# Slot means from column-tiled products, segments weighted ahead, and a written-out order of all instructions

## The chip, the cores and the metric

The kernel runs on one core of one Trainium2 chip. A core has five engines that run side by side and wait for one another through semaphores: TensorE (PE, matrix products and transposes; its weight loads are listed as PEld), VectorE (DVE), ScalarE (ACT), GpSimd (POOL) and SyncE (SP, which here only issues DMA transfers). The metric is the device time of one execution in microseconds. The median of three runs of the kernel before is 243.07 us (241.93 to 243.26).

## What is computed

```python
def mab(q, kv):                                   # softmax attention, one head
    s = scale * (q @ kv.transpose(0, 2, 1))
    s = s - s.max(-1, keepdims=True)
    a = np.exp(s)
    a /= a.sum(-1, keepdims=True) + 1e-09
    return a @ kv
h = mab(I, x)                                     # 32 inducing rows look at all of x
x = mab(x, h)                                     # every row of x looks at the 32 rows of h
...
logits = x @ phi                                  # 32 slots
d = softmax of logits over all rows               # (0)
slot_input = d.T @ x                              # 32 slot means
slot_out[e] = np.maximum(slot_input[e] @ w1[e], 0) @ w2[e]     # 8 experts, 4 slots each
c = softmax of logits over the 32 slots           # (1)
return c @ slot_out
```

x is 4 batches of 11456 rows of 128 numbers; the second part sees all 45824 rows as one. All is float32.

## The kernel before

**Tiles.** The rows of a batch are spread over 128 partitions, 90 blocks of 128 rows, and the blocks are cut into six tiles (five of 16 blocks, one of 10): 24 tiles, numbered 0 to 23, a multiple of six beginning a batch. A tile of scores is 128 partitions by 512 columns (320 for the small one): four groups of 32 partitions for the 32 inducing rows or slots, and blocks of 32 columns.

**Stages.** For each tile, group A (`group_a`) loads x (line 353) and, for 17 tiles, its transpose (line 361; for the other seven PE transposes, line 373, and ACT copies, line 381). It makes the scores of the inducing rows (`col_mm`, line 475), the running maximum (DVE line 394, ACT lines 400 and 402, a PE product with the matrix `rep`, line 407, DVE line 410), the exponentials (ACT line 415), turns them (DVE line 420, or PE and ACT in four tiles) and sums x with them (line 426: 16 products of 32 weight columns and 128 moving columns, four column tiles side by side). GpSimd rescales and adds these sums in `hz` (lines 436 and 444).

After the sixth tile of a batch `group_fin` finishes its mean: a product with `rep` that adds the four partition groups (line 482), the division on DVE (lines 486 to 488, which makes `h`), a transpose on PE (491), copies on ACT (494 and 497, `hts` and `ht`), and the product with phi (500, 504: `bdg`).

Group B (`group_b`) works on the batch's tiles again: scores against `hts` (line 475), softmax over 32 columns in `soft` (DVE transpose 523, maximum 527, POOL subtraction 531, ACT exponential 534, sums on POOL and DVE 539 to 558, POOL product 605, which gives `a2`), transpose (610), logits (613, put into `l_all` by lines 618 to 632). Three tiles form a segment, eight in all (`group_seg`): the segment's maximum (668 to 677), exponentials against it (688, with their sum in `z_l`), their transpose (694), and line 705, four products of 128 weight columns and 128 moving columns a tile, summed in PSUM tile `u` over the segment. Only its diagonal blocks of 32 by 32 are wanted: ACT copies `u` (722), POOL multiplies it by a mask (725; DVE 719 in the last segment), PE multiplies it by the batch mean `h` (728), ACT copies the result to `si_all` (731).

The small network (`group_mlp`) needs all eight segments: weights of the segments from their maxima (765, 768, 784), the denominator (772 to 792), the weights divided by it (795), eight products that add the weighted segments (801), the first layer (825: 32 products with 256 moving columns), the ReLU (831), two transposes (837, 842), the second layer (853: 64 products with 128 moving columns in two halves), a product with `rep` (863) and the copy to `srs` (866).

Group C (`group_c`) is the softmax of the logits over the slots, by `soft` again, with a transpose ahead (line 523, or in the seven tiles of list `TC` four transposes on PE, line 333, and a copy on ACT, line 336) and one behind (909). Group O (`group_o`) multiplies the slot outputs by it (926, four products a tile), copies the results (937, on ACT or DVE) and stores them (944).

**Order.** Everything is entered in a `Plan` with an engine, a cost in us and a priority. At build time `Plan.order` runs a list scheduler over this graph 24 times, forwards and backwards, keeps the order with the earliest end, and emits the instructions in it. So each engine's queue, SP's DMA queue among them, has a fixed order when the kernel runs. Warm-up products on PE fill gaps that the planner expects.

Of the kernel before, what the change touches and what calls it, by code (L numbers as in the profile page):

```python
# [8 lines left out]
F32 = mybir.dt.float32  # L9
# [6 lines left out]
S = 32  # L16
# [17 lines left out]
SEG = 3  # L34
NSEG = NT // SEG
# [5 lines left out]
}  # L41
LAG = {
    "ldn": -3.96, "ldt": -4.87, "tr": -1.2, "tre": 9.61, "a1": 0.0, "amx": -3.97, "am5": 0.0, "apm": 0.0, "ang": 2.71, "aex": -86.69, "aal": 0.3,
    "ate": 0.2, "a2": 0.4, "ahs": 5.38, "ahu": 0.6, "fin": -24.9, "b1": 9.19, "bts": 0.0, "bmx": 0.0, "bsb": 0.0, "bxp": 2.89, "bhf": 0.1,
    "bsm": 0.1, "bml": 0.2, "bta": 0.39, "c1": 0.36, "blm": 0.4, "ble": -7.69, "bch": -12.29, "bde": -24.64, "btd": -3.48, "c2": -44.1, "uf": 33.95,
    "warm": -2.57, "B": 18.08, "w": 29.25, "mlp": 8.95, "c": 70.84, "o": -0.67,
}
LAT = {("PE", "PE"): 0.0, ("ACT", "PE"): 0.27, ("DVE", "PE"): 0.26, ("DVE", "ACT"): 0.14, ("ACT", "DVE"): 0.1, ("DVE", "DVE"): 0.13, ("ACT", "ACT"): 0.05, ("Pool", "Pool"): 0.05}
LAT_OF = {"PE": 0.2, "DVE": 0.2, "ACT": 0.2, "Pool": 0.08, "DMA": 0.0}
DMA_LAT = 1.9  # L50
PASSES = 24
SEED = 0
NOISE = 0.0
BETA = 0.0
WARM = 8
WARM_PLAN = 2.3


def width(n):
    return SIZES[n % NCH] * S  # L60

# [13 lines left out]
TC = [1, 3, 6, 7, 9, 10, 15]  # L75
# [7 lines left out]

SLOPE = {"A": 0.574, "B": 0.622, "c": 0.566, "o": 2.276}


def first(p):

    return p[0] * SLOPE.get(p[1] if p[1] in SLOPE else "A", 1.0) + sum(LAG.get(x, 0.0) for x in p[1:])


ANY_ORDER = ("mm", "half")


class Plan:
# [3 lines left out]
    def __init__(self):  # L99
        self.ops, self.writers, self.readers, self.touch, self.rings = [], {}, {}, {}, {}  # L100

    def op(self, eng, cost, prio, fn, reads=(), writes=(), allocs=()):
        i = len(self.ops)
        deps = set()
        for k in reads:
            deps.update(self.writers.get(k, ()))
        for k in writes:
            deps.update(self.writers.get(k, ()))
            deps.update(self.readers.get(k, ()))
        for k in reads:  # L110
            self.readers.setdefault(k, []).append(i)
# [935 lines left out]
```

## Time and profile before

| what | us |
|---|---|
| median of three runs | 243.07 (241.93 to 243.26) |
| the profiled execution | 241.55 |
| its span, first to last instruction | 239.8 |
| busy in the span: PE, PEld | 201.4, 122.8 |
| busy in the span: DVE, ACT, POOL | 183.6, 147.0, 147.6 |
| read from HBM, written | 48.81 MB, 23.59 MB |

The profile is of one execution. Busy time of an engine is the union of its instructions. A float32 product shows as two instructions, each with a weight load of its own. The groups of instructions give a line, an engine, the tiles written and read, the shape, the count, the busy time and the mean length, and behind the second bar the idle time of the engine ahead of them and what ended it. The timeline merges like instructions that follow one another; its columns are start, length, and then the same names.

### The profile page before, as it was taken

The page shows a single profiled execution, that of the slowest core. Times are in us where ns is not written, and L with a number is a line of the kernel's source. Part 1 is how long each engine was busy: PE and PEld are TensorE (multiplying, and loading weights), DVE is VectorE, ACT ScalarE, POOL GpSimd, SP SyncE. Part 2 cuts the span into 40 slices and gives each one's busy share as a digit, 9 for nine tenths or more (in the row PEclk, how much of TensorE's full clock was granted, in tenths as well). Part 3 has the DMA queues.
Part 4 walks back from the last instruction along what each step waited for, and adds up shares of the span by engine and source line. Part 5 has one row for each costly group of instructions (what it writes and reads, how often), then busy time and mean ns, then how long its engine had stood idle before and what let it go on. Part 6 is the DMA issues. An engine that isn't in the chain of part 4 may idle for free.

```text
span 239.8 us, 5623 instructions
## 1 busy us (share of the span) xinstructions
PE 201.4 (84%) x2054; PEld 122.8 (51%) x2054; DVE 183.6 (77%) x427; ACT 147.0 (61%) x390; POOL 147.6 (62%) x237
## 2 busy tenths in 40 slices
PE   8899899699999799989999979989977968446370
PEld 8575574336655464637754654776843633211030
DVE  1125529879999699998969989994798999889650
ACT  2687594657747484586737652932259999285460
POOL 0001324979539697097961899986768887777810
PEclk9999999999999999999999999997999799575566
DMA  7999995999999969399996910000019999999977
GB/s 238 415 426 413 391 361 194 413 421 390 340 331 396 418 234 395 101 428 349 399 415 234 425 57 1 0 5 0 3 63 388 395 424 417 416 413 413 423 293 300
DMA packets 13851, 72.76 MB, mean 303 GB/s; under 512 B 1792, under 2 KB 2432, under 8 KB 6912
## 3 DMA queue, kind: packets, MB, share of 16 engines
q1 hardware_dynamic: 13392, 72.23, 76.6%
q8 instruction: 16, 0.26, 0.4%
q10 hardware_dynamic: 432, 0.18, 0.3%
q14 instruction: 11, 0.09, 0.1%
HBM read 48.81 MB, written 23.59 MB: 302 GB/s over the span
## 4 chain that ended last, share of the span: by engine, by line
PE 46%; DVE 15%; ACT 12%; DMA 10%; POOL 9%; issue 5%; ACTq 0%; POOLq 0%; SPq 0%
PE s L475 8%; DMA l_all<-xt 7%; PE po L926 7%; ACT ot L937 6%; PE ha L426 6%; PE lp L613 5%; PE tp L373 4%; PE s2p L475 4%; PE u L705 3%; DMA xt<-xt 3%; PE hpm L825 2%; ACT ct L534 2%; DVE l_all L909 2%; PE warm L317 2%; POOL ct L901 2%
## 5 line engine op out<-in xcount | busy, mean ns | idle before, releaser
L926 PE MATMUL po<-l_all,mb 32*128 32x512 f32 (+1 forms) x192 | 37.6, 783 | 16.1 <-DVE l_all L909 13.2
L937 ACT COPY ot<-po 128x512 f32<-128x512 f32 (+1 forms) x71 | 34.8, 594 | 16.8 <-PE po L926 16.4
L531 POOL TENSOR_TENSOR bt<-bt,bm 128x512 f32<-128x512 f32 (+1 forms) x24 | 23.7, 994 | 20.5 <-DVE bm L527 20.1
L926 PEld LDWEIGHTS po<-l_all,mb 32*128 32x128 f32 x192 | 17.2, 236 | 34.9 <-issue 13.6
L531 POOL TENSOR_TENSOR ct<-ct,cm 128x512 f32<-128x512 f32 (+1 forms) x24 | 23.8, 993 | 11.5 <-DVE cm L527 7.1
L705 PE MATMUL u<-d,a 128*128 128x128 f32 (+1 forms) x184 | 25.4, 281 | 0.4 <-DVE d L694 0.4
L901 POOL TENSOR_TENSOR ct<-ct,cz 128x512 f32<-128x512 f32 (+1 forms) x24 | 23.8, 1001 | 2.7 <-DVE cz L558 2.4
L705 PEld LDWEIGHTS u<-d,a 128*128 128x128 f32 (+1 forms) x184 | 22.3, 189 | 4.9 <-issue 1.0
L605 POOL TENSOR_TENSOR a<-bt,bz 128x512 f32<-128x512 f32 (+1 forms) x24 | 23.9, 995 | 1.5 <-DVE bz L558 1.2
L613 PE MATMUL lp<-a2t,bdg 128*128 128x512 f32 (+1 forms) x48 | 24.0, 594 | 0.9 <-ACT a2t L336 0.6
L394 DVE TENSOR_REDUCE m<-s 128x1 f32<-128x512 f32 (+1 forms) x24 | 15.3, 639 | 11.9 <-PE s L475 11.7
L426 PEld LDWEIGHTS ha<-xn,e 128*32 128x32 f32 x668 | 18.5, 110 | 9.0 <-issue 6.2
L426 PE MATMUL ha<-xn,e 128*32 128x128 f32 x668 | 22.8, 274 | 0.0
L436 POOL TENSOR_TENSOR hz<-hz,al 128x129 f32<-128x129 f32 x20 | 8.0, 398 | 23.2 <-ACT al L433 22.4
L475 PE MATMUL s<-xt,it_sb 128*32 128x512 f32 (+1 forms) x152 | 19.2, 577 | 2.4 <-DMA xt<-xt 1.2
L534 ACT ACTIVATE ct<-ct 128x512 f32<-128x512 f32 (+1 forms) x24 | 15.0, 629 | 9.5 <-POOL ct L531 9.5
L534 ACT ACTIVATE bt<-bt 128x512 f32<-128x512 f32 (+1 forms) x24 | 14.4, 600 | 10.3 <-POOL bt L531 10.1
L909 DVE STREAM_TRANSPOSE l_all<-ct 128x512 f32<-128x512 f32 (+1 forms) x24 | 16.0, 668 | 4.1 <-POOL ct L901 4.1
L937 DVE COPY ot<-po 128x512 f32<-128x512 f32 (+1 forms) x25 | 16.0, 645 | 3.5 <-PE po L926 3.4
L415 ACT ACTIVATE et<-s,negm 128x512 f32<-128x512 f32 (+1 forms) x24 | 15.7, 656 | 4.7 <-DVE negm L410 3.9
L688 ACT ACTIVATE dt<-l_all,negm_l 128x512 f32<-128x512 f32 (+1 forms) x24 | 16.5, 687 | 3.2 <-DVE negm_l L677 2.9
L475 PE MATMUL s2p<-xt,hts 128*32 128x512 f32 (+1 forms) x152 | 17.6, 573 | 0.0
(174 smaller groups left out, 428.2 us busy)
## 6 DMA issues: line engine op xcount, KB each, us to landing
xn<-xn SPq DMA_DIRECT2D x18, 1024.0 KB, 7.1
out<-ot SPq DMA_DIRECT2D x13, 1024.0 KB, 8.6
xt<-xt SPq DMA_DIRECT2D x11, 1024.0 KB, 8.7
w<-w SPq DMA_DIRECT2D x8, 1024.0 KB, 7.5
out<-ot SPq DMA_DIRECT2D x16, 256.0 KB, 2.8
l_all<-xt SPq DMA_DIRECT2D x3, 1024.0 KB, 8.2
out<-ot SPq DMA_DIRECT2D x6, 512.0 KB, 4.1
xt<-xt SPq DMA_DIRECT2D x3, 640.0 KB, 6.0
```

Source lines behind the costliest of these rows:

```text
L426: nc.tensor.matmul(ha[32 * q : 32 * q + 32, :P], T["e1", a][:, j * S : (j + 1) * S], T["xn", a][:, j * P : (j + 1) * P], start=j < 4, stop ...
L475: nc.tensor.matmul(dst[32 * g : 32 * g + 32, :w], lhs, src, start=True, stop=True)
L531: nc.gpsimd.tensor_tensor(tv, tv, T[k("m")][:, :nb].unsqueeze(2).broadcast_to(full), op=ALU.subtract)
L534: nc.scalar.activation(T[k("t")][:, :w], T[k("t")][:, :w], AF.Exp)
L605: nc.gpsimd.tensor_tensor(blocks(a2), blocks(t), zb, op=ALU.mult)
L613: nc.tensor.matmul(ptile("mm", ("lp", n))[:, :w], T["bdg", b], T["a2t", n][:, :w], start=True, stop=True)
L688: nc.scalar.activation(dt_[:, :v], l_of(n)[:, :v], AF.Exp, bias=negm_l[:, k : k + 1], accum_out=z_l[:, k, i : i + 1])
L705: nc.tensor.matmul(u[:m, :m], a2[:, o : o + m], d[:, o : o + m], start=i == 0 and o == offs[0], stop=i == SEG - 1 and o == offs[-1],)
L901: nc.gpsimd.tensor_tensor(blocks(t), blocks(t), zb, op=ALU.mult)
L909: nc.vector.transpose(l_of(n), T["ct", n][:, :w])
L926: nc.tensor.matmul(T["po", 4 * n + g][:, :w], T["srs",][q, :], l_of(n)[q, :], start=True, stop=True)
L937: (nc.vector.tensor_copy if dve else nc.scalar.copy)(ot[:, g * w : (g + 1) * w], T["po", m][:, :w])
```

## The change

- Line 705's product is now 16 products a tile, each with 32 weight columns and 32 moving columns, that write the wanted 32 by 32 blocks alone, into four column tiles that add up over the tile's blocks and the segment. `u` is then 128 by 32. Mask, masked copies, the product with `h` for each segment and `si_all` are gone; ACT copies `u` to `us_all` (segments 0 to 6).
- In the small network the first seven segments are weighted against their own common maximum while the eighth is still under way (e1 to e8): weights, their spread over partitions by a product with a matrix of ones, the product with `us_all`, and seven products with the `h` of the batch, added up. The last segment joins by two weights (g1 to g8). The slot means so come from two products (g7a, g7b). The denominator now divides the slot outputs in the copy to `srs` (gs) and no longer the weights.
- The first layer is split in two halves of 128 moving columns (64 products), each with a ReLU and a transpose of its own; both layers are entered in parts of six and two experts.
- `group_fin`: the sum of the denominators has its own short path (f0 to f2), the division goes into a scaled copy of `rep` (f2b), and two products with it give the transposed mean at once (f3a, f3), one from the sum of five tiles, one from the sixth tile's part. `h` is made later by a transpose and a copy (f8, f9). The GpSimd addition of the sixth tile is gone.
- In batch 0 the running maximum of group A is on DVE (one step a tile) and no longer on ACT.
- `TC` is gone: all 24 tiles of group C are transposed by DVE. The new modes of `soft` (lists `BV` to `CB`) are empty.
- `Plan` keeps only the functions; `ORDER`, a list of 1297 numbers, is the order in which they are emitted, and `WARMS` says after which of them how many warm-up products follow (ten places, 20 products in all). Ring sizes, semaphores and transfers are as before but for small tiles.

```diff
 def c2(n=n, i=i):
...
-                offs = list(range(0, w, P))
...
-                    nc.tensor.matmul(
-                        u[:m, :m], a2[:, o : o + m], d[:, o : o + m],
-                        start=i == 0 and o == offs[0], stop=i == SEG - 1 and o == offs[-1],
-                    )
+                for j in range(nb):
+                    q = slice(32 * (j % 4), 32 * (j % 4) + 32)
+                    c = slice(j * S, j * S + S)
+                    nc.tensor.matmul(u[q, :S], a2[:, c], d[:, c], start=i == 0 and j < 4, stop=i == seg - 1 and j >= nb - 4)
...
-        op("PE", 0.23, pr, f1, [("hz", b)], [("hp", b)], [("mm", ("hp", b))])
-        op("DVE", 0.65, pr, f2, [("hp", b)], [("h", b)], [("h", ("h", b))])
-        op("PE", 0.11, pr, f3, [("h", b)], [("htp", b)], [("mm", ("htp", b))])
+        op("DVE", 0.07, pr, f0, [("zc", a5), ("hz", b)], [("zt", b)])
+        op("PE", 0.22, pr, f1, [("zt", b)], [("hp", b)], [("mm", ("hp", b))], ni=4)
+        op("DVE", 0.22, pr, f2, [("hp", b)], [("rz", b)])
+        op("ACT", 0.25, pr, f2b, [("rz", b)], [("rzr", b)], [("rzr", ("rzr", b))])
+        op("PE", 0.28, pr, f3a, [("hz", b), ("rzr", b)], [("htp", b)], [("mm", ("htp", b))], ni=4)
+        op("PE", 0.28, pr, f3, [hl, ("rzr", b)], [("htp", b)], ni=4)
...
+            if mv and c:
+                nc.vector.scalar_tensor_tensor(m5[:, 0:4], mask4, T["m1", a], T["m5", a - 1][:, 0:4], op0=ALU.mult, op1=ALU.max)
+                return
...
+        def e5b():
+            nc.tensor.matmul(ptile("ha", ("wr",))[:, : K * S], ones, T["wsel",][:S, : K * S], start=True, stop=True)
+        def e5c():
+            nc.vector.tensor_tensor(T["uss",][:, : K * S], us_all[:, : K * S], T["wr",][:, : K * S], op=ALU.mult)
+        def e7():
+            sip = ptile("mm", ("sip",))
+            for t in range(K):
+                nc.tensor.matmul(sip[:, :S], T["h", SEG_AT[t] // NCH], T["uss",][:, t * S : (t + 1) * S], start=t == 0, stop=t == K - 1)
...
+        def g7a():
+            nc.tensor.matmul(ptile("mm", ("sit",))[:, :S], ident, T["sis",], start=True, stop=False)
+        def g7b():
+            nc.tensor.matmul(T["sit",][:, :S], T["h", B - 1], T["uss",][:, last], start=False, stop=True)
...
+        def g9(k, es):
+            def f():
+                hp = T["hpm", k] if es[0] else ptile("mm", ("hpm", k))
+                for e in es:
+                    for q in range(4):
+                        nc.tensor.matmul(
+                            hp[32 * q : 32 * q + 32, :P], T["z1s",][:, 32 * e : 32 * e + 32], wslice(1, e * F + (2 * q + k) * P, P),
+                            start=e == 0, stop=e == E - 1,
+                        )
+            return f
...
         def gs():
-            nc.vector.tensor_copy(T["srs",], T["sr",][:, :P])
+            nc.vector.tensor_scalar_mul(T["srs",], T["sr",][:, :P], T["rz", "l"])
...
-    order = plan.order()
-    T["plan"] = plan
     with tc.manual_schedule():
-        for i, gap in plan.gaps(order):
-            plan.ops[i][3]()
-            if gap > 0.5 and ("warm1",) in T and ("po", 0) not in T:
-                warm(("warm1",), int((gap - 0.3) / 0.215))
+        for i in ORDER:
+            plan.ops[i]()
+            if i in WARMS:
+                warm(("warm1",), WARMS[i])
```

More of the change, by code (lines that the diff above doesn't have):

```diff
@@ L1 @@
 import math
-import random
 import concourse.bass as bass
@@ L33 @@
 TB = [14, 15, 18, 19]
-SEG = 3
-NSEG = NT // SEG
+SEGS = [3, 3, 3, 3, 3, 3, 3, 3]
+SEG = max(SEGS)
+NSEG = len(SEGS)
+SEG_AT = [sum(SEGS[:k]) for k in range(NSEG)]
 RINGS = {
@@ L38, with seg_of, whole @@
     "dt": 2, "d": 3, "a2": 6, "mm": 4, "s2p": 3, "s1": 2, "u": 1, "ha": 1, "xa": 1, "xb": 1,
[2 rows of a table removed]
-}
[L42 to L54, printed above, removed]
[1 row of a table added]
+}
 WARM = 8
-WARM_PLAN = 2.3
 def width(n):
     return SIZES[n % NCH] * S
+def seg_of(n):
+    k = max(k for k in range(NSEG) if SEG_AT[k] <= n)
+    return k, n - SEG_AT[k]
+def whole(n):
+    return SIZES[n % NCH] % 4 == 0
 def valid(n):
@@ L402, in am5 @@
                 nc.scalar.mul(m5[:, 4:5], nmask0, T["negm1", b][:, c - 1 : c])
-        n5 = 5 if c else 4
+        mv = a - c in MV
+        n5 = 5 if c and not mv else 4
         def apm():
@@ L592, in pr @@
             return n, "B", o
+        mode = mode_of(n, BV, BE, BP) if whole(n) else "T"
+        turned = mode != "T"
         def b1():
-            col_mm(ptile("mm", ("s2p", n)), T["hts", b], n)
+            sp = ptile("mm", ("s2p", n))
+            col_mm(sp, T["hts", b], n)
         w = width(n)
@@ new lines, in group_mlp @@
+        op("ACT", 0.2, pe, e2, [("nmp",)], [("wl",)])
+        op("DVE", 0.09, pe, e3, [("wl",)] + [("z", n) for n in range(SEG_AT[K])], [("zw",)])
+        op("DVE", 0.09, pe, e3b, [("zw",)], [("zs",)])
+        op("DVE", 0.32, pe, e5, [("wl",), ("mb",)], [("wsel",)])
+        op("PE", 0.35, pe, e5b, [("wsel",), ("mb",)], [("wr",)], [("ha", ("wr",))], ni=4)
+        op("DVE", 0.32, pe, e5c, [("wr",), ("mb",)] + [("us", k) for k in range(K)], [("uss",)])
+        op("PE", 0.2 * K, pe, e7, [("uss",), ("mb",)] + [("h", SEG_AT[k] // NCH) for k in range(K)], [("sip",)], [("mm", ("sip",))], ni=4 * K)
@@ new lines, in group_mlp @@
+        op("ACT", 0.1, pe, e8, [("sip",)], [("sis",)])
+        ul = ("us", "last")
+        op("DVE", 0.07, pr, g1, [("ngl", K), ("nmp",)], [("nm",)])
+        op("ACT", 0.2, pr, g2, [("nm",)], [("wl2",)])
+        op("DVE", 0.09, pr, g5, [("wl2",)], [("ws2",)])
+        op("PE", 0.24, pr, g5b, [("ws2",)], [("wr2",)], [("ha", ("wr2",))], ni=4)
+        op("ACT", 0.1, pr, g5d, [("wr2",), ("mb",)], [ul])
+        op("DVE", 0.09, pr, g5f, [("wr2",)], [("sis",)])
+        op("PE", 0.25, pr, g7a, [("sis",)], [("sit",)], [("mm", ("sit",))], ni=4)
@@ L878, in group_mlp @@
         op("DVE", 0.07, pr, g6b, [], [("rz",)])
[L879 to L884 removed]
+        parts = (range(0, 6), range(6, E))
```

518 lines of the change are left out of this document (236 added, 282 removed), and 62 rows, old and new, of tables (ORDER, RINGS).

## Prediction

> **What bounds the kernel now.** I read the page first, then a table of busy times by stage, then the timeline around the two joints between stages, then groups and waits. The page's totals and slices:
>
> ```profile
> PE 201.4 (84%) x2054; PEld 122.8 (51%) x2054; DVE 183.6 (77%) x427; ACT 147.0 (61%) x390; POOL 147.6 (62%) x237
> PEclk9999999999999999999999999997999799575566
> DMA  7999995999999969399996910000019999999977
> ```
>
> PE is the fullest engine on average, but the DMA row shows three different stages: transfers almost without a pause while the tiles are loaded, none for five slices, then transfers without a pause while the output is written. The table by stage (columns: PE, PEld, DVE, ACT, POOL busy, granted clock, DMA share, GB/s):
>
> ```profile
> 0.00:40.00 40.00, 36.84 (x421) 25.40 (x421) 14.78 (x34) 25.59 (x70) 5.57 (x16) 1.00 0.90 349
> 40.00:120.00 80.00, 74.07 (x954) 44.32 (x953) 72.82 (x175) 52.13 (x164) 58.15 (x100) 1.00 0.92 354
> 120.00:152.00 32.00, 30.01 (x202) 17.87 (x198) 28.51 (x75) 17.82 (x46) 23.51 (x35) 1.00 0.53 211
> 152.00:163.20 11.20, 9.91 (x79) 9.01 (x79) 9.51 (x28) 5.10 (x17) 9.05 (x14) 1.00 0.01 3
> 163.20:176.25 13.05, 11.82 (x211) 8.20 (x210) 8.94 (x23) 4.45 (x8) 9.18 (x14) 0.87 0.01 3
> 176.25:228.00 51.75, 34.24 (x180) 16.27 (x184) 46.01 (x94) 37.84 (x79) 41.13 (x58) 0.77 0.96 389
> 228.00:239.80 11.80, 4.46 (x24) 1.77 (x24) 3.07 (x6) 4.12 (x9) 0.98 (x2) 0.64 0.76 295
> ```
>
> Two things follow. First, the first output product starts at 176.25 (its row stands below) and the span ends at 239.8, so 63.55 us follow it, with DMA at 0.96 for most of them: the output stage is paced by its stores, and the end moves with the moment T at which the output can start. Second, from 40 to 163 both PE and DVE are over nine tenths busy. DVE's work cannot be handed over by this change, so I set up the sum on DVE: T is the time that DVE works ahead of T plus the time that it idles ahead of T. Its idle time by stage is 25.2, 7.2, 3.5, 1.7 and 4.1 us, 41.7 in all, beside 134.6 us of work. A faster PE helps only as far as it takes away this idle time.
>
> **The change part by part.** *The product of the second mean* (line 705). Today 24 tiles take four 128x128 products each:
>
> ```profile
> 40.00:120.00 80.00, 12.97 (x92) 11.29 (x92) 0.00 (x0) 1.02 (x4) 1.00 0.92 354
> 64.33 1.06 PE L426 MATMUL ha<-xn,e 128*32 128x128 f32 x32
> 65.63 1.14 PE L705 MATMUL u<-d,a 128*128 128x128 f32 x8
> 66.70 0.64 PE L475 MATMUL s2p<-xt,hts 128*32 128x512 f32 x4
> 160.83 1.97 PE L801 MATMUL sit<-mb,si_all 128*128 128x32 f32 x16 [0.66 <-DVE mb L795]
> 128.57 0.16 PEld L475 LDWEIGHTS s2p<-xt,hts 128*32 128x32 f32 x8 [0.17 <-issue]
> ```
>
> One tile (8 instructions, two to a product) takes 66.70-65.63 = 1.07 us with its start, and the first row has twelve such tiles' worth of work (92 instructions, 12.97 us) in the stage from 40 to 120. The new form has 16 products a tile with 32 weight columns and 32 moving columns, four column tiles side by side. No row has this. The nearest row above is line 426: the same 16 column-tiled products, 32 instructions, with four times the moving columns, 1.06 us. That would be no gain. From below, line 801 has 32 moving columns behind 128 weight columns, 1.97/16 = 0.123 us an instruction, which the weights set; with a quarter of the columns it is 0.031, and 32 instructions take 0.98 us one behind another and 0.25 us four abreast. The last row speaks for abreast: eight such loads lie in 0.16 us. I take 0.45 us, nearer the low end for that row, with ends of 0.25 and 1.06. Relief of PE: 12 x 0.6 = 7 us from 40 to 120, and as much again up to 160.
>
> The Trainium skill ("TensorE: Matmul & The Clock Gate", the section on the 56 ns gap) states that start-to-start of matmuls never drops below about 25 ns however small they are. By that rule 32 instructions take at least 0.80 us, the relief is 12 x 0.27 = 3 us, and the sum below would give an estimated 241.2, between the forecast and the first rival. No run here shows it: the 33 ns an instruction of line 426 lie above it.
>
> *What hangs on that product.* Gone are seven masked copies on POOL, eight products with the batch mean (two instructions each), eight copies on ACT, and at the end the eight products of line 801. (The last three rows below count what lies ahead of 176.25 alone.)
>
> ```profile
> L725 POOL TENSOR_TENSOR um<-us,mask_bd 128x128 f32<-128x128 f32 x7 | 3.2, 460 | 0.3
> L728 PE MATMUL sip<-h,um 128*128 128x128 f32 x16 | 3.0, 288 | 0.2 <-DVE um L719 0.2
> L795 DVE TENSOR_SCALAR mb<-mb,rz_l 128x256 f32<-128x256 f32 x1 | 1.2, 1218 | 0.0
> L784 DVE TENSOR_TENSOR mb<-cst,wl 128x256 f32<-128x256 f32 x1 | 0.6, 590 | 0.0
> L488 DVE TENSOR_SCALAR h<-hp,rz 128x128 f32<-128x128 f32 x4 | 1.4, 351 | 0.1
> L668 DVE TENSOR_TENSOR m4b<-mx,cst 128x12 f32<-128x12 f32 x8 | 2.0, 256 | 0.0
> ...
> L527 DVE TENSOR_REDUCE cm<-ct 128x16 f32<-128x512 f32 (+1 forms) x10 | 6.4, 643 | 0.5 <-ACT ct L336 0.5
> L523 DVE STREAM_TRANSPOSE ct<-l_all 128x512 f32<-128x512 f32 (+1 forms) x5 | 3.2, 648 | 0.0
> L558 DVE RECIPROCAL cz<-cz 128x16 f32<-128x16 f32 (+1 forms) x9 | 2.0, 227 | 0.9 <-POOL cz L555 0.8
> ```
>
> DVE loses lines 795, 784 and 488, 1.2+0.6+1.4 = 3.2 us. It gains the weights of seven segments and their product (two by line 784, 1.1 us), six running maxima of the first batch, four sums of batch totals and some eight small steps (18 by about 0.2, line 668 being the upper end: 3.6 us, of which 3 ahead of T), and *seven transposes that PE made* (list TC): 7 x 0.65 = 4.6 us. Counting the table's entries, nine tiles are turned on DVE ahead of the last copy of the slot means, where the trace has five, so four of the seven count ahead of T: 2.6 us. One row maximum and one reciprocal fewer come ahead of T: -0.9. Work ahead of T: -3.2+1.1+3+2.6-0.9 = +2.6. As the small steps stand at their upper end, I take +1.8 (ends +0.8 and +2.6). Behind T: three transposes, the maximum and the reciprocal put off, 2.0+0.9 = +2.9.
>
> *The joint at 122* (batch mean). The denominator gets a path of its own, ahead of the last product, and normalising moves into a product.
>
> ```profile
> 121.87 0.85 PE L426 MATMUL ha<-xn,e 128*32 128x128 f32 x20
> 123.52 0.46 POOL L444 TENSOR_TENSOR hz<-hz,hs 128x129 f32<-128x129 f32 x1
> 125.89 0.35 DVE L488 TENSOR_SCALAR h<-hp,rz 128x128 f32<-128x128 f32 x1
> 127.83 0.20 ACT L494 ACTIVATE hts<-htp 128x32 f32<-128x32 f32 x1
> 128.58 0.64 PE L475 MATMUL s2p<-xt,hts 128*32 128x512 f32 x4
> ```
>
> From the last product's end (122.72) to the first score product of the last batch (128.58) are 5.9 us, through ACT, POOL, PE, DVE, PE and ACT. The new path keeps a copy on ACT, two products that each take one weight load, and the copy on ACT, with another tile's product and copy queued between by the table: about 3 us. The 3 us saved are worth at most the stage's DVE idle time. The same step shortens batch 0, where DVE idles from 0 to 40 for want of scores.
>
> *The layers of the small network.*
>
> ```profile
> 163.20 5.35 PE L825 MATMUL hpm<-w,ma 128*32 128x256 f32 x64
> 164.00:165.00 1.00, 1.00 (x16) 0.49 (x12) 1.00 (x3) 0.47 (x1) 0.53 (x2) 0.50 0.00 0
> 170.02 1.96 PE L853 MATMUL so<-w,ma 128*32 128x128 f32 x64
> 171.79 1.93 PE L853 MATMUL so<-w,mb 128*32 128x128 f32 x64
> 175.38 0.49 PE L863 MATMUL sr<-sos,cst 128*128 128x128 f32 x2 [1.07 <-DVE sos L860]
> 176.25 0.71 PE L926 MATMUL po<-l_all,mb 32*128 32x512 f32 x4 [0.16 <-DVE mb L866]
> ```
>
> The first layer took 5.35 us, and the granted clock was 0.50 in its middle. Split in halves of 128 columns it has the instructions of the second layer twice, 2 x 1.9 = 3.8 us at full clock, 5.4 if the clock falls again for as long. I take 5.4: PE ahead of it does thinner work than before. The 1.5 us between the layers (168.55 to 170.02) shrink, since the first half's activation and transpose run under the second half. From 163.20 to 176.25 are 13.05 us; new: 5.4+0.2+3.8 and 2.0 of the 2.5 us that today lie between the second layer's end (173.72) and 176.25, 11.4.
>
> *Moved.* All instructions come in a new order on every queue, SP's included. Loads wait for buffers that PE frees:
>
> ```profile
> SPq L361 <- PE s2p L475: 26.3, 10, 7.3
> ```
>
> so a relieved PE lets loads go sooner; the counts and sizes of the transfers stay. ACT and POOL lose more than they get, and bind nowhere ahead of T. In the table warm-up products stand at ten places; they cost PE little where it waits.
>
> **The sum.** Work of DVE ahead of T: +1.8. Idle: 0 to 40, 25.2 to 24.2 (-1.0; ends 0, -2); 40 to 120, 7.2 to 4.7 (-2.5: a third of PE's relief, for DVE is at 91% already; ends 0, -5); 120 to 152, 3.5 to 2.0 (-1.5; ends 0, -2.5); 152 to T, 5.8 to 4.3 (-1.5: by the 1.6 us of the small network; ends +1, -3). T moves by 1.8-6.5 = -4.7, to 171.6. Behind T, DVE gets 2.9 us more in a stage where it idles 51.75-46.01 = 5.7:
>
> ```profile
> 226.96 0.71 DVE L909 STREAM_TRANSPOSE l_all<-ct 128x512 f32<-128x512 f32 x1 [0.68 <-POOL ct L901]
> 229.50:231.30 1.80, 1.80 (x12) 0.55 (x7) 1.11 (x2) 1.46 (x3) 0.09 (x1) 0.50 0.14 57
> ```
>
> The stores already run dry once, for 1.8 us, because the last tiles' softmax comes late; I let that hole grow by 1.0 (ends 0 and 2.9). The span goes to 239.8-4.7+1.0 = 236.1. The profiled execution took 241.55, 1.75 more than its span, so 237.85, and the median of the runs (243.07) stands 0.6% over the profiled execution: 239.4 us. The ends of the terms add up to -11.7 and +6.5.
>
> **Rivals.** *First: PE is not relieved.* If the thin products take about 1 us, the terms of 40 to 120 and of the first half of the late stages (2.5+0.7) fall away: 239.4+3.2 = 242.6, no change that a measurement of this kernel can tell (0.5% is about what it can tell). For it: line 426 as it stands. Against: the eight loads in 0.16 us.
>
> *Second, slower: DVE becomes the wall.* If its idle time ahead of T is waiting for loads and POOL rather than for PE, the turned transposes and small steps add up without return: +2.6 ahead of T and +2.9 behind it, 248.6. It decides once DVE from 40 to 152 is over 95% busy while T has not moved; a middle case, with half of the idle time given back, is +1.8-3.2+2.9, 244.6. For it: the 91% above. Against: PE's own 93% there, with the batch joint visibly serial.
>
> *Third: the clock.* With thin products PE may be granted 0.50 through both layers: 3.8 more in the second layer and 2.2 more in the first, 6.0 on top of the forecast, 245.4, and it decides when the granted clock is under 0.7 from 163 to T. Against: the second layer ran at full clock behind a halved first.
>
> The Trainium skill (the same page, Part 1 on the clock gate) says that a window of some 3.4 us with an idle PE brings the clock to half. The row with 0.50 agrees with the half; an idle PE stood not ahead of it, for from 152 to 163.2 it was busy for 9.91 of 11.2 us.
>
> *Fourth: the order is much better than the planner's,* since it isn't bound to a rule: idle of 40 to 152 down to 2 us gives 234 or less.
>
> **Chances.** Forecast 0.50, with its neighbours from 236 to 241.8; fourth rival 0.15; first 0.15; second and third together 0.20, of which 0.03 end within the half per cent. Faster 0.65, same 0.18, slower 0.17. The range leaves out the far ends of fourth and second: 233.5 to 245.5.
>
> **What would show it.** Right: line 705's successor under 0.6 us a tile; from 40 to 152 PE clearly under 90% busy and DVE over 93%; the first output product at 170 to 173; about 64 us from there to the end. Wrong: that product near 1 us a tile; DVE as idle as before; T where it was; the layers at half clock; or a hole in the stores of over 4 us.

## The result, and the profile after

The kernel after takes 235.19 us (median of four runs, 233.12 to 237.61) against 242.50 of the kernel before on the same chip (241.33 to 243.26); the ratio is 0.967, 95% interval 0.957 to 0.978. The forecast was 239.4 with a range of 233.5 to 245.5, faster at 0.65. So sign and range held, and the gain is 7.3 us where about 3.7 were forecast. Runs of both kernels spread by 2% and more on some chips, and the ratios leave disturbed executions out, so they differ a little from those of the medians.

The profiled execution of after took 233.12 us, its span is 231.3. First the totals of its page, the granted clock and the DMA share by fortieths:

```profile
PE 195.4 (84%) x2658; PEld 108.7 (47%) x2658; DVE 188.9 (82%) x445; ACT 144.1 (62%) x376; POOL 143.3 (62%) x227
PEclk9999999999999999998599999999999995555555
DMA  7999996999999999999478950000059999999987
```

PE lost 6 us, DVE gained 5.3, and DVE's share of a shorter span went from 77% to 82%. Then the table by stage, in the columns of the prediction (stretch, its length; PE, PEld, DVE, ACT, POOL busy; granted clock, DMA share, GB/s), cut at the start of the first layer and at the first output product:

```profile
0.00:40.00 40.00, 36.31 (x416) 24.91 (x417) 17.10 (x41) 23.69 (x60) 6.57 (x18) 1.00 0.91 357
40.00:120.00 80.00, 74.97 (x1220) 41.19 (x1220) 74.92 (x179) 55.14 (x169) 57.43 (x96) 0.96 0.93 368
120.00:152.00 32.00, 29.54 (x457) 16.50 (x456) 31.75 (x83) 17.65 (x47) 25.74 (x38) 1.00 0.46 170
152.00:157.46 5.46, 5.16 (x114) 4.44 (x113) 5.46 (x19) 3.16 (x11) 3.34 (x8) 1.00 0.01 5
157.46:167.37 9.91, 9.44 (x266) 8.09 (x267) 9.09 (x26) 2.70 (x6) 8.33 (x12) 1.00 0.02 4
167.37:219.50 52.13, 34.98 (x172) 12.48 (x176) 47.41 (x97) 37.59 (x77) 40.22 (x58) 0.72 0.96 386
219.50:231.30 11.80, 5.05 (x24) 1.06 (x20) 3.19 (x7) 4.21 (x9) 1.69 (x3) 0.50 0.78 299
```

The first output product (the moment T of the prediction) comes at 167.37 in place of 176.25, 8.9 us sooner. From there to the end are 63.9 us, as before (63.55). So all of the gain lies ahead of T. DVE's idle time there, the length of a stretch less its DVE column, is now 22.9, 5.1, 0.25, 0.0 and 0.8 us, 29.05 in place of 41.7; its work is 167.37-29.05 = 138.3 in place of 134.6. From 120 us to T, DVE has hardly a gap left: 46.30 us of work in 47.37.

The timeline shows the three places on which the forecast was built. The product of the second mean, for one tile, for two tiles that follow one another, and its group (count, busy us, mean ns | idle before, releaser):

```profile
118.12 0.46 PE L716 MATMUL u<-d,a 128*32 128x32 f32 x32
149.22 0.94 PE L716 MATMUL u<-d,a 128*32 128x32 f32 x64
L716 PE MATMUL u<-d,a 128*32 128x32 f32 x720 | 10.6, 201 | 0.8 <-DVE d L706 0.4
```

A tile takes 0.46 us with its start, in place of 1.07, or 0.94/64 = 0.015 us an instruction.

The joint between the last batch's mean and its first scores:

```profile
122.55 0.85 PE L349 MATMUL ha<-xn,e 128*32 128x128 f32 x20
124.43 0.46 PE L425 MATMUL htp<-rzr,hz 128*128 128x128 f32 x2
124.73 0.39 PE L428 MATMUL htp<-rzr,hs 128*128 128x128 f32 x2
125.81 0.64 PE L401 MATMUL s2p<-xt,hts 128*32 128x512 f32 x4
```

From the end of the last product (123.40) to the scores (125.81) are 2.4 us in place of 5.9, with products of two other tiles' logits (line 619) in between.

And the small network:

```profile
157.46 3.27 PE L864 MATMUL hpm<-w,ma 128*32 128x128 f32 x112
161.03 0.64 PE L864 MATMUL hpm<-w,ma 128*32 128x128 f32 x16
161.49 1.49 PE L893 MATMUL so<-w,ma 128*32 128x128 f32 x48
163.17 0.65 PE L893 MATMUL so<-w,ma 128*32 128x128 f32 x16
163.94 1.96 PE L893 MATMUL so<-w,mb 128*32 128x128 f32 x64
166.44 0.49 PE L903 MATMUL sr<-sos,cst 128*128 128x128 f32 x2
167.37 1.14 PE L1007 MATMUL po<-l_all,mb 32*128 32x512 f32 x8 [0.22 <-DVE mb L906]
```

The first layer takes 3.27+0.64 = 3.9 us, the second runs right behind it, and the granted clock is 1.00 throughout: 9.91 us in place of 13.05.

### The profile page after: what moved, and what is told of

Its sections match the earlier page's. It is cut to its first block, busy times and chain, and to the rows that moved or that the text cites. A ratio compares the mean times of both kernels' runs of the same rounds, so it can differ in the third digit from the quotient of the medians.

```text
span 231.3 us, 6816 instructions
## 1 busy us (share of the span) xinstructions
PE 195.4 (84%) x2658; PEld 108.7 (47%) x2658; DVE 188.9 (82%) x445; ACT 144.1 (62%) x376; POOL 143.3 (62%) x227
## 4 chain that ended last, share of the span: by engine, by line
PE 37%; DVE 27%; DMA 15%; POOL 7%; ACT 6%; issue 4%; SPq 1%; ACTq 0%; DVEq 0%; POOLq 0%
PE po L1007 8%; PE s L401 7%; PE ha L349 5%; PE s2p L401 5%; ACT ot L1017 4%; DMA xt<-xt 4%; DMA l_all<-xn 4%; DMA xn<-xn 4%; DVE l_all L978 4%; PE lp L619 4%; PE tp L291 3%; DMA l_all<-xt 3%; DVE ct L476 2%; POOL a L596 2%; POOL ct L959 2%
## 5 line engine op out<-in xcount | busy, mean ns | idle before, releaser
L1007 PE MATMUL po<-l_all,mb 32*128 32x512 f32 (+1 forms) x192 | 40.0, 821 | 18.6 <-DVE l_all L978 12.2
L1007 PEld LDWEIGHTS po<-l_all,mb 32*128 32x128 f32 x192 | 13.5, 239 | 44.4 <-DVE l_all L978 22.6
L619 PE MATMUL lp<-a2t,bdg 128*128 128x512 f32 (+1 forms) x48 | 25.5, 624 | 0.3 <-DVE a2t L616 0.2
L349 PE MATMUL ha<-xn,e 128*32 128x128 f32 x668 | 23.1, 275 | 0.4 <-PE pmb L686 0.3
L401 PE MATMUL s<-xt,it_sb 128*32 128x512 f32 (+1 forms) x152 | 20.5, 615 | 2.3 <-DMA xt<-xt 1.4
L401 PE MATMUL s2p<-xt,hts 128*32 128x512 f32 (+1 forms) x152 | 18.1, 573 | 0.2 <-DVE bt L476 0.2
L343 DVE STREAM_TRANSPOSE e<-et 128x512 f32<-128x512 f32 (+1 forms) x20 | 13.1, 653 | 6.3 <-ACT et L338 6.3
L476 DVE STREAM_TRANSPOSE bt<-s2p 128x512 f32<-128x512 f32 (+1 forms) x24 | 15.6, 658 | 1.1 <-PE s2p L401 1.1
```

Source lines behind the costliest of these rows:

```text
L349: nc.tensor.matmul(ha[32 * q : 32 * q + 32, :P], T["e1", a][:, j * S : (j + 1) * S], T["xn", a][:, j * P : (j + 1) * P], start=j < 4, stop ...
L401: nc.tensor.matmul(dst[32 * g : 32 * g + 32, :w], lhs, src, start=True, stop=True)
L476: nc.vector.transpose(make(), src())
L619: nc.tensor.matmul(ptile("mm", ("lp", n))[:, :w], T["bdg", b], T["a2t", n][:, :w], start=True, stop=True)
L1007: nc.tensor.matmul(T["po", 4 * n + g][:, :w], T["srs",][q, :], l_of(n)[q, :], start=True, stop=True)
```

## The experiments

The theory from the two profiles: PE's relief is a condition of the gain and not the gain. The idle time of DVE goes away because the written-out order uses what PE gives, and most of it goes where the planner's order left several engines waiting for one another. The rivals: the thinner product does it by itself; the shorter joint and the split layer do it; warm-ups and the clock do it.

All profiles beside one another. "Scores" is the start of the last batch's first score product; idle is DVE's, by the stretches 0–40, 40–120, 120–152 and 152–T; times in us.

| kernel | median (range) | ratio to before, interval | scores | T | DVE work to T | idle | T to end |
|---|---|---|---|---|---|---|---|
| before | 242.50 (241.33–243.26) | | 128.6 | 176.25 | 134.6 | 25.2, 7.2, 3.5, 5.8 | 63.5 |
| after | 235.19 (233.12–237.61) | 0.967, 0.957–0.978 | 125.8 | 167.37 | 138.3 | 22.9, 5.1, 0.3, 0.8 | 64.0 |
| e1_wide | 237.60 (236.56–238.19) | 0.982, 0.974–0.989 | 126.8 | 172.40 | 139.5 | 22.6, 5.1, 2.1, 3.1 | 64.0 |
| e2_thin_old | 248.87 (246.89–250.47) | 1.026, 1.016–1.036 | 135.1 | 182.29 | 135.5 | 27.5, 10.2, 2.1, 7.0 | 66.4 |
| e3_planner | 238.46 (236.49–239.47) | 0.985, 0.976–0.993 | 129.6 | 173.50 | 136.4 | 24.8, 8.2, 1.0, 3.1 | 64.1 |
| e4_no_warm | 233.39 (232.59–237.84) | 0.964, 0.955–0.972 | 122.9 | 166.68 | 138.4 | 23.1, 2.0, 0.7, 2.5 | 64.1 |
| e8_thin_same | 243.71 (242.53–244.70) | | 127.9 | 177.28 | 134.4 | 25.7, 6.7, 3.0, 7.5 | 63.5 |
| e5_tc | 240.23 (235.40–240.57) | | 124.6 | 172.59 | 137.0 | 22.7, 4.7, 0.9, 7.4 | 66.2 |
| e6_unsplit | 235.21 (234.59–241.27) | | 122.4 | 168.09 | 138.2 | 22.6, 2.2, 0.2, 4.8 | 64.7 |
| e7_old_mean | 236.92 (234.52–240.76) | | 125.6 | 170.77 | 137.3 | 23.7, 4.0, 1.5, 4.4 | 64.6 |
| e9_after | 234.69 (232.64–237.69) | 0.975, 0.967–0.983 | 124.4 | 168.38 | 138.5 | 24.0, 2.6, 0.3, 3.0 | 64.8 |
| e11_more_warm | 231.92 (230.98–232.94) | 0.966, 0.960–0.971 | 122.0 | 165.00 | 138.2 | 22.5, 2.0, 0.7, 1.7 | 66.1 |
| e12_less_dve | 231.76 (230.45–235.54) | 0.959, 0.953–0.964 | 122.9 | 165.88 | 138.3 | 22.9, 2.3, 0.7, 1.7 | 63.7 |

The kernels e1 to e4 shared one chip (before: 241.18), e5 to e8 another (before: 243.38, 238.4 to 246.0), e9 to e11 a third (before: 244.27, 239.41 to 246.76), e12 a fourth (before: 241.84). Medians are compared within a group. The columns from "scores" on are of one profiled execution each, and the granted clock in it is not the same in all.

### The wide product in the new kernel

```diff
-                for j in range(nb):
-                    q = slice(32 * (j % 4), 32 * (j % 4) + 32)
-                    c = slice(j * S, j * S + S)
-                    nc.tensor.matmul(u[q, :S], a2[:, c], d[:, c], ...)
+                for o in offs:
+                    m = min(P, w - o)
+                    nc.tensor.matmul(u[:m, :m], a2[:, o : o + m], d[:, o : o + m], ...)
```

> The changed kernel with the product of the second mean put back to four 128x128 products a tile, order and all else as in the change. (It leaves out that off-diagonal blocks are masked: columns 0 to 31 of the wide product are copied.) If PE's relief makes the gain, about 0.6 us comes back on PE for each of 24 tiles, 14 us in all, and the start of the output moves from 167.4 to 172 or later, the time to 240 or more. If it is the new order that keeps DVE busy, PE has room for most of it: T moves by less than 2 us and the time stays under 237.

Measured: 237.60 us, 4.2 over e4_no_warm, which is the kernel after but for its warm-ups and ran on the same chip (233.39). Its table by stage, and the group of the product:

```profile
40.00:120.00 80.00, 76.43 (x948) 44.55 (x952) 74.90 (x177) 53.60 (x168) 56.52 (x95) 1.00 0.93 362
120.00:152.00 32.00, 30.40 (x232) 19.66 (x223) 29.88 (x78) 16.84 (x44) 24.48 (x37) 1.00 0.46 173
152.00:172.40 20.40, 19.65 (x344) 17.23 (x344) 17.35 (x50) 6.67 (x20) 13.63 (x21) 1.00 0.01 3
L718 PE MATMUL u<-d,a 128*128 128x128 f32 (+1 forms) x184 | 25.7, 282 | 0.6 <-DVE d L706 0.4 <-ACT d L254 0.2
```

The product is back at 25.7 us in all, 15 us more than the thin one, and 4 to 6 of them arrive at T. They show in 120 to 152 (DVE idle 2.1 us) and from there to T (3.1), where PE is busy for 19.65 of 20.40 us. In the new order the relief counts for a quarter to two fifths of its size.

### The thin product in the old kernel

The same edit the other way round in the kernel before, once with the planner told the new cost (0.02+0.38 us a tile), once with the old cost left in, which leaves its order as it was (the masked copies then read the narrow block four times). The line on the cost is changed in the first of the two alone:

```diff
-            op("PE", 0.87 * w / 480, pr("c2"), c2, ...)
+            op("PE", 0.02 + 0.38 * w / 512, pr("c2"), c2, ...)
```

> The kernel before with the thin column-tiled product alone; masked copy on POOL (now from 32 columns), product with the batch mean and the planner stay, with 0.40 us as the planner's cost of the product. If PE's relief makes the gain, 3 us or more are gained by this alone (239.5 or less where the kernel before has 242.5). If the order makes it, the old planner wins under 1.5 us by it.

> As the thin product in the kernel before, but the planner is told the old cost of the product (0.93 us), so that it makes the very order of the kernel before. If the loss of the other run came from the order that the planner made of the new cost, this one is no slower than the kernel before, and by the relief of PE 2 to 4 us faster. If the thin product itself delays something (PSUM, weight loads), it is slower here too.

With the old order the thin product gains nothing: 243.71 us beside 243.38 of the kernel before (the quickest executions took 242.53 and 238.40), and T comes at 177.28.

```profile
40.00:120.00 80.00, 70.65 (x1228) 38.68 (x1225) 73.35 (x177) 52.29 (x165) 58.56 (x102) 0.98 0.93 360
120.00:152.00 32.00, 28.67 (x364) 15.28 (x363) 28.97 (x75) 18.12 (x46) 23.90 (x36) 0.95 0.51 204
152.00:177.28 25.28, 21.19 (x390) 16.22 (x391) 17.79 (x46) 8.55 (x23) 17.65 (x27) 0.80 0.01 3
```

PE is busy for 70.65 us from 40 to 120, where it was busy for 74.07: 3.4 us of relief show there, and they have become waiting of PE. DVE's idle time is nearly what it was (6.65 and 3.03 against 7.18 and 3.49); that the queues still meet at the same places is the likely reason, not a shown one. So the rival that the thinner product does it by itself falls, up to 152 us. Behind that the granted clock is 0.80 in this profile and 0.93 in that of before, and DVE idles 1.7 us more. All four executions with the thin product have a lower mean clock than those of the kernel before on the same chip (0.890 to 0.905 against 0.910 to 0.924). What the thin product would bring at a full clock there is not shown.

With the new cost the planner finds another order, and the kernel is 2.6% slower than before (T at 182.29). Its first scores of batch 0 come at 38.4 us in place of 36.1. The planner's estimate of its own orders doesn't rank them as the chip does.

### The planner in place of the table

All new operations of the kernel after, ordered by the list scheduler of before:

```diff
-        for i in ORDER:
-            plan.ops[i]()
-            if i in WARMS:
-                warm(("warm1",), WARMS[i])
+        for i, gap in plan.gaps(order):
+            plan.ops[i][3]()
+            if gap > 0.5 and ("warm1",) in T and ("po", 0) not in T:
+                warm(("warm1",), int((gap - 0.3) / 0.215))
```

> All operations of the changed kernel, but the order made by the list scheduler of the kernel before, with its priorities and warm-up rule, instead of the table. If the operations make the gain, it stays under 237. If the table makes it, it goes to 240 or more, with DVE idle for 5 us more ahead of the output.

Measured: 238.46 us, 0.985 of before; the kernel with the table stands at 233.39 to 235.19.

```profile
40.00:120.00 80.00, 71.72 (x1121) 38.49 (x1121) 71.81 (x172) 52.72 (x164) 55.10 (x91) 0.96 0.92 348
120.00:152.00 32.00, 30.02 (x441) 18.85 (x441) 31.05 (x84) 17.53 (x48) 26.38 (x42) 1.00 0.52 199
152.00:173.50 21.50, 20.06 (x482) 16.90 (x479) 18.36 (x52) 7.89 (x23) 14.55 (x21) 0.84 0.01 4
```

From 40 to 120, DVE idles for 8.2 us, 1.0 more than before the change, although PE is busy for only 71.7 of the 80 us; the clock of 0.96 there may have a part in it. On one chip, against e4_no_warm, giving up the table costs 5.1 us and giving up the thin product 4.2, of 7.8 in all. They add up to more than the whole: without the table 2.7 us of the gain are left, without the thin product 3.6, and each works in part through the other. The table without the new operations was not tried, as it is a list of these operations.

### The warm-up products left out

```diff
-WARMS = {822: 9, 740: 1, 641: 2, 643: 1, 791: 1, 864: 2, 842: 1, 876: 1, 897: 1, 899: 1}
+WARMS = {}
```

> The changed kernel without the 20 warm-up products of its ten places. If they keep the clock up (my third rival, turned round), the granted clock falls to 0.5 for a window or more between 130 and 167, the two layers (7.5 us in the change) take 9 to 11, and the time rises by 2 to 4 us. If PE's own products are enough, the time stays within 1 us.

Measured: 233.39 us, 0.964 of before, no slower than the kernel after (0.967). In its profile the clock was 0.77 from 152 us to T, and T still came at 166.68. The 20 products bring nothing that shows.

### Seven turns back on PE and ACT

```diff
+TC = [1, 3, 6, 7, 9, 10, 15]
...
+            if pre == "c" and n in TC:
+                ...
+                for q in range(4):
+                    nc.tensor.transpose(pt[:, q * P : (q + 1) * P], src()[:, q * P : (q + 1) * P], ident)
+                nc.scalar.copy(dst, pt)
```

> The changed kernel with seven of group C's turns put back on PE and ACT at the same places of the table (as in list TC of the kernel before). DVE is busy for 99% from 120 to 167, so 0.65 us of DVE fall away for each, four ahead of the output. If DVE is the bound there, T moves 1.5 to 2.5 us ahead and the time falls by 1 to 3 us. If the turns' waits on PE and ACT take it back, it stays or rises.

Measured: 235.40, 239.93, 240.53 and 240.57 us. The quickest lies beside those of e6_unsplit (234.59) and e7_old_mean (234.52) in the same group, so neither a loss nor a gain is shown. The profile is of the 240.57. In it DVE's work to T is 1.3 us less than in after, and its idle time from 152 to T is 7.4, with PE busy for 19.57 of 20.59 us there at a clock of 0.75; whether the turns or the clock made that idle time stays open. The order was not remade for it either.

### The first layer undivided, and the old batch mean

```diff
+                if k == 0:
+                    return
+                hp = T["hpm", 0] if es[0] else ptile("mm", ("hpm", 0))
...
-                            hp[32 * q : 32 * q + 32, :P], T["z1s",][:, 32 * e : 32 * e + 32], wslice(1, e * F + (2 * q + k) * P, P),
+                            hp[32 * q : 32 * q + 32, :FQ], T["z1s",][:, 32 * e : 32 * e + 32], wslice(1, e * F + q * FQ, FQ),
```

> The changed kernel with the first layer undivided: 32 products with 256 moving columns, then one ReLU, and transpose and copy of the first half behind it. The transposes are no longer hidden: about 1.2 us more between the layers. If the network's chain sets T, the time rises by 1 to 1.5 us; if DVE sets it (0.8 us idle in 9.9 us there), by the difference only, 0.3 to 0.7 us.

```diff
         def f3a():
-            nc.tensor.matmul(ptile("mm", ("htp", b))[:, :P], T["hz", b][:, :P], T["rzr", b], start=True, stop=False)
+            nc.gpsimd.tensor_tensor(T["hz", b], T["hz", b], T[hl], op=ALU.add)
+            hp = ptile("mm", ("hp", b))
+            nc.tensor.matmul(hp[:, : P + 1], rep, T["hz", b], start=True, stop=True)
+            ...
+            nc.vector.tensor_scalar_mul(stile("h", ("h", b), P, 4), hp[:, :P], rz)
```

> The changed kernel with the old path of the batch mean (addition on POOL, sum with rep, division on DVE, transpose on PE) at the place of the new products in the table. I had put the new path at 3 us less at the last batch's joint and 1.5 us of DVE's idle time. Three us at each joint should show as 1.5 to 4 us more; if DVE is kept busy by other work from the table, under 1 us.

The undivided layer takes 235.21 us and the old mean 236.92, on the chip with the wide spread. The undivided layer's own profile has T at 168.09, 0.7 behind that of after, with the clock at 0.79 from 152 us on; what the split saves is not to be told from the clock. The old mean has T at 170.77, 3.4 behind, all of it after the last batch's scores (45.2 us from there to T against 41.6), with the clock at 0.73 from 152 us on. Both effects are within what this group's spread can hide, and neither size is settled.

### A faster clock in the output stage

In the profile of after the clock is 0.50 from 190 us to the end. Six dummy products ahead of each output product from tile 12 on, with the kernel after run beside it:

```diff
+            if n >= 12:
+                for _ in range(6):
+                    nc.tensor.matmul(T["po", 4 * n][:, :P], wz, wz, start=True, stop=True)
             for g in range(4):
                 q = slice(32 * g, 32 * g + 32)
                 nc.tensor.matmul(T["po", 4 * n + g][:, :w], T["srs",][q, :], l_of(n)[q, :], start=True, stop=True)
```

> The kernel after, unchanged, as the reference of this group of runs. From its earlier four runs (0.967 of the kernel before, 233.1 to 237.6 us): 0.960 to 0.975 of the kernel before on this chip, first output product at 167 to 170 us, and about 64 us from there to the end of the span.

> The kernel after, with six dummy products (128 moving columns, into a bank that the output product then overwrites) ahead of each output product from tile 12 on, to see what the half clock costs there: in the profile of the kernel after the granted clock is 0.50 from 190 us to the end. If the stores alone pace the output stage: the same as the reference within 0.5%, with 64 us from the first output product to the end, whatever the clock. If the half clock delays the last tiles (the DMA share falls to 0.78 in the last 12 us): the clock is higher from 190 us on and the stage is 0.5 to 2 us shorter. If the dummies are in the way of the products: 0.5 to 2 us longer.

The kernel after came out at 0.975 (0.967 to 0.983), T at 168.38 and 64.8 us behind it, as expected. The one with dummies has a ratio of 0.976 (0.966 to 0.985): the same. In five of its six executions the mean granted clock was 0.945 to 0.971, against 0.884 to 0.894, and they took 233.58 to 239.38 us. So the clock went up, and nothing came of it: the stores pace that stage, or the dummies cost what the clock brings. The sixth execution, the one with the profile, took 463 us and says nothing on this; it is told of below.

### More warm-ups, then less work on DVE at the end

```diff
-WARMS = {822: 9, 740: 1, 641: 2, 643: 1, 791: 1, 864: 2, 842: 1, 876: 1, 897: 1, 899: 1}
+WARMS = {822: 9, 740: 1, 641: 2, 643: 1, 791: 1, 864: 3, 842: 3, 876: 2, 897: 1, 899: 1, 649: 1, 784: 1, 793: 2, 796: 2, 871: 1}
```

> The kernel after, with 36 warm-up products in place of 20, the new ones around the last segment and the two layers. If the spread of the kernel after (233.1 to 237.6 us) comes from granted half clock that falls into the layers or not, as PE looks idle or not ahead of them: the clock from 152 us to the first output product is 1.00 in the profile, the median falls by 1 to 3 us against the reference and the spread narrows. If the clock there does not follow from PE's idle time: the same median within 0.5%, the same spread, and the layers now and then at half clock. Without any warm-up products the kernel was already as fast (0.964 of the kernel before), which speaks for the second.

The numbers in the edit come to 31 warm-up products, 11 more than in after, and not to the 36 that the expectations name. Measured: 231.92 us against 234.69 of after in the same group, and all six executions within 230.98 to 232.94, where after spread from 232.64 to 237.69. The last stretch ahead of T, first of after (e9_after) from 152 to 160 us and on to 170, then of this kernel to its T:

```profile
152.00:160.00 8.00, 8.00 (x157) 7.10 (x160) 6.87 (x20) 2.02 (x8) 5.02 (x8) 0.57 0.02 5
160.00:170.00 10.00, 9.66 (x242) 7.44 (x230) 8.15 (x22) 2.70 (x6) 6.46 (x10) 1.00 0.01 2
```

```profile
152.00:165.00 13.00, 12.55 (x365) 10.79 (x364) 11.30 (x34) 2.92 (x6) 10.16 (x15) 1.00 0.02 4
```

The clock is 1.00 up to T, as expected. But the cause of the 2.8 us is not settled by that. The added products all stand behind the start of the last batch's scores, and there this profile is already 2.4 us ahead (122.02 against 124.39), with 1.6 us less idle time of DVE from 0 to 40 us, where the clock of e9_after was 0.96; only 1.0 of the 3.4 us at T arise behind it. In the first profile of after the clock was full without them, and there those 41.6 us from scores to T are the shortest of all. What the runs show is a better median and a narrower spread in one group; that the clock is what does it is argued only.

Of the 3.4 us at T, 2.0 arrive at the end: the stores run dry sooner. Three output copies moved from DVE to ACT, tiles 16, 18 and 19:

```diff
-OD2 = [2, 3, 5, 6, 7, 8, 9, 10, 12, 14, 15, 16, 18, 19, 20, 21, 23]
+OD2 = [2, 3, 5, 6, 7, 8, 9, 10, 12, 14, 15, 20, 21, 23]
```

> The kernel with 36 warm-up products, with three output copies (tiles 16, 18 and 19) moved from DVE to ACT at the same places in the order. In the profile with 36 warm-ups the first output product came at 165.0 us, 3.4 ahead of the reference, but the end came only 2.0 us ahead: the stores ran at a DMA share of 0.89 from 200 to 220 us against 0.98, with DVE busy for 16.6 of those 20 us and ACT for 11.7. If the softmax of the last tiles on DVE paces that stretch, 3 x 0.65 = 1.95 us less work there brings the DMA share back to 0.95 or more, from the first output product to the end are 64 to 65 us in place of 66.2, and the time is 0.955 to 0.962 of the kernel before. If PE at half clock or ACT paces it: the same 66 us, and 0.962 to 0.970. In both cases the clock from 152 us to the first output product is 1.00 and the runs lie within 1% of each other, if the added warm-ups do what the earlier group of runs showed.

The stretch from 200 to 220 us, with the added warm-ups and then with the copies moved as well:

```profile
200.00:220.00 20.00, 11.02 (x51) 3.12 (x48) 16.64 (x35) 11.72 (x23) 16.01 (x22) 0.50 0.89 366
```

```profile
200.00:220.00 20.00, 12.26 (x52) 3.54 (x56) 15.70 (x32) 13.07 (x27) 15.90 (x23) 0.50 0.97 401
```

The DMA share goes from 0.89 to 0.97 with the clock at 0.50 in both, and from T to the end are 63.7 us in place of 66.1. This is what was expected if DVE holds the stores there, but it does not show it. The profiles of after and e4_no_warm have 64.0 and 64.1 us behind T with the three copies on DVE, and e9_after, also with them, has in the same stretch:

```profile
200.00:220.00 20.00, 11.19 (x48) 2.95 (x48) 17.38 (x36) 12.10 (x24) 16.20 (x22) 0.59 0.98 405
```

There DVE is busier than in either, and the DMA share is 0.98. So the 66.1 us of e11_more_warm stand out, and what made them is open. The time of e12_less_dve is 0.959 of before (0.953 to 0.964), the lowest ratio of all kernels here, though its interval overlaps that of e11_more_warm, on another chip. One of the six executions took 235.54, so the narrow spread did not hold in full.

## Why the prediction was right in sign and short in size

*The lens held.* T moved by -8.9 us, the output stage behind it kept its length (+0.4; forecast +1.0), and T is DVE's work plus DVE's idle time: +3.75 and -12.65. The forecast was +1.8 and -6.5. The idle time is the step that failed: its terms behind 120 us were too small (-8.2 measured, -3.0 forecast). The work was off the other way.

*The thin product* was rightly priced: 0.45 us forecast, 0.46 measured. The first rival, that PE is not relieved, put 3.2 us on it; e1_wide shows 4.2 in the new order. The estimate by the Trainium skill ("TensorE: Matmul & The Clock Gate", the section on the 56 ns gap) of at least 0.80 us a tile is not borne out: 64 instructions in 0.94 us start 15 ns after one another on average, below its 25 ns. Four column tiles run side by side here, so in each of them it is one start in some 59 ns; the rule may hold for each, but not for the engine.

*"A third of PE's relief"* (40 to 120) failed as a way of reckoning. The size came near in the profile shown (-2.1 against -2.5), and the same order reaches -4.6 to -5.2 in e9, e4, e11 and e12, where DVE idles for 2.0 to 2.6 us. But the third is no property of the relief. In the old order it is nothing (e8: -0.5), and with the planner's order of the new operations DVE idles more than before (e3: 8.2). The order decides how much of a relief arrives, and the clock has a part in it: of the 5.1 us that DVE idles in the profile of after, 3.1 lie from 105 to 115 us.

```profile
105.00:110.00 5.00, 2.90 (x42) 1.27 (x42) 4.03 (x12) 2.63 (x10) 4.27 (x8) 0.84 1.01 407
110.00:115.00 5.00, 5.00 (x54) 2.40 (x53) 2.88 (x7) 3.12 (x10) 2.14 (x4) 0.50 0.54 226
```

In e9, e4, e11 and e12, at a clock of 1.00 there, DVE idles for 0 to 0.8 us in the same stretch. DVE waits for PE in it (lines 333 and 310 of after). So that this term came near the forecast is probably luck: a fall of the clock that the forecast did not have seems to have taken back some 3 us (an estimate from these rows) of what the order gave.

*120 to 152 and 152 to T* were the terms most too small in this profile: -3.2 and -5.0, where -1.5 and -1.5 were forecast. The first repeats: 0.25 to 0.7 us of idle time are left in all five profiles of the table's order with the product and layers as in after (after, e4, e9, e11, e12). The second is 1.7 to 3.0 us in the others, so the profile shown is the best of them, and -3 to -4 is the fair size. Two parts of it can be named. The network took 9.9 us, 1.5 less than forecast, since I let the clock fall in the first layer and it did not in this execution. And DVE works for 9.09 of these 9.91 us, where it worked for 8.94 of 13.05: the table puts softmax work of the output stage into the gaps of the network. This is the fourth rival (idle from 40 to 152 down to 2 us; 2.7 to 5.3 were measured; by the terms of the sum it would end at 239.4-4.7 = 234.7, not at the 234 that I wrote). I gave it 0.15, with a table in the diff that was bound to no rule, and it deserved more.

*The joint at 122* came out as said: 2.4 us for a forecast of about 3.

*DVE's work* is +3.75, beyond my upper end of 2.6. Two terms were mis-sized. The first is a count: ten tiles are turned on DVE ahead of T against five, not nine:

```profile
L476 DVE STREAM_TRANSPOSE ct<-l_all 128x512 f32<-128x512 f32 x9 | 6.3, 698 | 0.0
L476 DVE STREAM_TRANSPOSE ct<-l_all 128x320 f32<-128x320 f32 x1 | 0.5, 467 | 0.0
L680 DVE TENSOR_TENSOR m4b<-mx,cst 128x12 f32<-128x12 f32 x8 | 3.3, 412 | 0.0
L411 DVE TENSOR_TENSOR zt<-hz,hs 128x1 f32<-128x1 f32 x4 | 2.5, 618 | 1.2 <-POOL hz L359 1.2
```

The first two come to 6.75 us (9 x 0.698 + 0.467) against 5 x 0.648 = 3.24 in the row of before, +3.5 for a forecast of +2.6. The second is in the last two rows. I had put the small steps at 0.2 us each, below the mean of 0.26 in the row that I called their upper end; the sums of one number to a partition (zt) took 0.62, and line 680, which the change doesn't touch, went from 2.0 to 3.3 us in all. These excesses are lengths, and the lengths of DVE's instructions overlap: all of them ahead of T add up to 161.13 us in place of 155.37, 5.76 more, of which 3.75 are left as busy time. The timeline says why the small steps grew; here are the first sum and the last, with what GpSimd does:

```profile
30.55 0.40 POOL L359 TENSOR_TENSOR hz<-hz,al 128x129 f32<-128x129 f32 x1
30.98 0.16 DVE L411 TENSOR_TENSOR zt<-hz,hs 128x1 f32<-128x1 f32 x1 [1.18 <-POOL hz L359]
...
121.12 1.05 POOL L495 TENSOR_TENSOR ct<-ct,cm 128x512 f32<-128x512 f32 x1
121.26 0.92 DVE L411 TENSOR_TENSOR zt<-hz,hs 128x1 f32<-128x1 f32 x1
```

With GpSimd idle the step takes 0.16 us. With GpSimd at work it ends at 122.18, right behind GpSimd's end at 122.17. The same holds for the two others that took long: they end with a GpSimd operation, within 0.03 us. The Trainium skill ("SBUF — State Buffer", the section on the two separate sides) states it: an operation of VectorE with two inputs in SBUF and a GpSimd operation that reads SBUF hold a shared pair of ports by turns, each for a whole instruction. The trace agrees (122.18 behind 122.17), and the trace of before already held it, in the row whose mean I took:

```profile
67.14 0.13 DVE L668 TENSOR_TENSOR m4b<-mx,cst 128x12 f32<-128x12 f32 x1
...
147.35 1.05 POOL L531 TENSOR_TENSOR ct<-ct,cm 128x512 f32<-128x512 f32 x1
...
147.45 0.97 DVE L668 TENSOR_TENSOR m4b<-mx,cst 128x12 f32<-128x12 f32 x1
```

The same step took 0.13 us alone and 0.97 us behind GpSimd. I read its mean of 0.26 and not its spread.

*The signs I named.* Under 0.6 us a tile, DVE over 93% from 40 to 152 (95%) and about 64 us behind T were right. "PE clearly under 90% busy" was wrong: it is at 93% as before (104.5 of 112 us), for the freed time holds other work sooner. The first output product came ahead of the 170 to 173 that I gave.

*The other rivals.* DVE is now the wall: it was said to decide at 95%, and DVE is at 95 to 98% from 40 to 152 in these profiles. Yet T moved, since the work it gained was less than the idle time it lost. The clock (third rival) does fall into the layers in some executions: 0.57 from 152 to 160 us in e9_after. That one took 2.4 us longer from the last scores to T than the profile at full clock (44.0 against 41.6), so the 6.0 us of the rival would need the half clock in all of it. It also came where the rival did not look, at 110 us in the profile of after. That profile was unlucky there and lucky behind 152, by some 3 and 2 us as estimated from these rows.

## What to carry to other kernels

A relief on one engine can be worth nothing by itself in a kernel whose queues have a fixed order (243.71 us beside 243.38 here): try it once in the old order, and count the gain of the new order and of the new operation separately, knowing that they overlap. Reckon a late moment as one engine's work plus its idle time by stage; ask for each stage whether the idle time could be filled at all, and give that case weight when the change brings a new order. Read the spread of a small step's durations and not only its mean: here a step of 0.16 us on VectorE took up to 0.92 us when it had to wait out a GpSimd operation. And look at the clock of each stretch before an idle time is put down to an order.

## What the runs showed of the hardware

*Half clock with a busy PE.* From 152 to 160 us in e9_after the granted clock was 0.57 with PE busy for 8.00 of 8.00 us. From 105 to 110 us PE was busy for 2.90 of 5.00 us in after, where the clock then fell to 0.50, and for 2.74 of 5.00 in e9_after, where it stayed at 1.00. Busy time in these profiles doesn't tell whether the clock will be kept.

*One execution at half pace.* The profiled execution of e10_out_clock took 463 us. Its score products, in the row below it those of e9_after:

```profile
L401 PE MATMUL s<-xt,it_sb 128*32 128x512 f32 (+1 forms) x152 | 45.7, 1302 | 0.7 <-ACT xt L299 0.7
```

```profile
L401 PE MATMUL s<-xt,it_sb 128*32 128x512 f32 (+1 forms) x152 | 20.0, 599 | 2.2 <-DMA xt<-xt 1.3
```

They take 1302 ns in place of 599, from the first tiles on, long ahead of the dummies, while the profile gives a granted clock of 1.00 and DVE, ACT and GpSimd keep their durations within some per cent (1.05 us for GpSimd's 128x512 operation in both). PE was slow in a way that this clock does not show. It was seen once, and the cause is open.
